# Splitting GpSimd's late bonus products by heads, and summing the last tile's left 256 columns ahead of the right 128

## The chip, the cores and the metric

The kernel runs on one core of one Trainium2 chip. The metric is the time of one execution on the device in microseconds, the median of several runs. A profiled execution shows for each engine what ran when; its span is counted from the first recorded instruction to the last and is a little shorter than the time of a run. TensorE (PE in the profile) multiplies matrices, with weight loads listed apart (PEld); VectorE is DVE, ScalarE is ACT, GpSimd is POOL, and SyncE is SP, here the queue that issues transfers.

## The reference

Two stages follow each other. The first is a linear attention with a decaying state, for 4 sequences of 768 steps, 8 heads of 48 elements:

```
cur = einsum('bhd,bhe->bhde', u * k[t], v[t])
y[t] = einsum('bhd,bhde->bhe', r[t], state + cur)
state = w[t][..., None] * state + einsum('bhd,bhe->bhde', k[t], v[t])
```

The term with u is the bonus of the current step. It can be pulled out of the recurrence: for each step and head it is v[t] times one number, the sum over d of r u k. The second stage is a feed-forward layer on the 3072 rows of 384 columns that come out: h = x @ w_in with 2048 columns, a leaky ReLU with slope 0.01, and g @ w_out back to 384 columns.

## The kernel before, in words

The steps are cut into 24 chunks of 128 (six for each sequence). A chunk's attention is done in parallel form: VectorE, ScalarE and GpSimd make decayed copies of r and k (rk), these are transposed (rkT), TensorE makes scores of 128x128 for each head (L787), VectorE masks them (m, L459), and TensorE sums scores times v and the state's part in a PSUM bank, yp (L817 and L822). Beside this runs the bonus (L402 to L421): ru is r times u (L408), then that times k (L412), VectorE reduces it over each head to dg, one number for each of 8 heads (L416), and the bonus product vs is v times dg spread over 48 elements (L420). All elementwise products go through the helper at L334, which sends them to VectorE or GpSimd. At L490 VectorE adds yp and vs to y, which is transposed into xT (from chunk 12 on by a transfer, L496).

The second stage goes chunk by chunk too. Up: four times 12 matmuls of 128 columns, into a PSUM bank hp (L860), then ScalarE's leaky ReLU to g (L907). Down: four quarters of four matmuls of 384 columns into a PSUM bank op (L928). A copy to o follows on ScalarE or VectorE (L964), and a transfer to the output (L968).

The last chunk, number 23, is special. Its sum lies in two banks: op holds the left 256 columns, and yp, by then free of attention, the right 128 (`last_parts`, L873). In the first three quarters the loop at L926 to L930 does a left and a right matmul in turn for each of four rows of the weights. The fourth quarter is written in two steps (L935 to L944): four left matmuls, then four right ones. Behind each part follows a copy, on ScalarE for the left and on VectorE for the right (L945), and a transfer from SyncE (L950 to L953).

The order in which each engine executes its instructions is fixed in advance. Every piece of work is a step with an engine, a duration that the planner assumes, dependencies and a priority. A planner (`Plan.order`, L40) simulates the engines with these durations and gives out the steps in order of their start; a list written by hand (EARLY, L162) fixes the order of the attention's steps on each engine, and for some of them the engine. P0 is ten times the number of the chunk (L718). Steps with several instructions keep these together. Waits between engines are put in from the data that the instructions touch. Buffers go round in rings: four of vs, three of dg, two of hp.

Of the kernel before, what the change touches and what calls it, by code (L numbers as in the profile page):

```python
# [126 lines left out]
def kernel(  # L127
# [106 lines left out]
    w_out_b = pool.tile([128, NJ, DM], BF16, name="w_out_b")  # L234
# [29 lines left out]
    with tc.manual_schedule():  # L264
# [52 lines left out]
        def step(eng, dur, fn, pri, reads=(), writes=(), deps=(), wire=None, rows=0, **alts):  # L317

            d = list(deps)
            for x in writes:  # L320
                d += x.old
            i = plan.add(eng, dur, fn, d, pri, wire, rows, {eng: dur, **alts} if alts else None)
            for x in (*reads, *writes):
                x.steps.append(i)
            return i

        def copy(e, o, i):
            if e == "ACT":
                nc.scalar.copy(out=o, in_=i)  # L329
            else:  # L330
                (nc.vector if e == "DVE" else nc.gpsimd).tensor_copy(out=o, in_=i)  # L331

        def times(e, o, a, b):
            (nc.vector if e == "DVE" else nc.gpsimd).tensor_tensor(out=o, in0=a, in1=b, op=ALU.mult)  # L334
# [4 lines left out]
        def act(n, src=180):  # L339
            return (src + n) / 1200.0 + 0.02  # L340
# [55 lines left out]
        def product(rk, a, xn, e, P0, deps, banked):  # L396
# [2 lines left out]
                lambda eng: times(eng, rk.t[:, a, :, 0:D], xn.t, e.t[:]),  # L399
                P0, reads=[xn, e], writes=[rk], deps=deps, **({"DVE": 0.58} if banked else {"POOL": 1.05}))  # L400

        def bonus(vs, rn, kn, vn, loads, P0):  # L402

            ru, dg = ru_r.take(), dg_r.take()
            kl, rl, vl = loads
            s_ru = step(
                "POOL", 1.05,
                lambda e: times(e, ru.t[:], rn.t, ubv),  # L408
                P0 + 2, reads=[rn], writes=[ru], deps=[rl, u_ld], DVE=0.84)
            s_ruk = step(  # L410
                "POOL", 1.05,
                lambda e: times(e, ru.t[:], ru.t[:], kn.t),  # L412
                P0 + 2, reads=[kn, ru], deps=[kl, s_ru], DVE=0.84)
            s_dg = step(
                "DVE", 0.54,
                lambda: nc.vector.tensor_reduce(out=dg.t[:], in_=ru.t[:], axis=AX.X, op=ALU.add),  # L416
                P0 + 2, reads=[ru], writes=[dg], deps=[s_ruk])
            return step(
                "POOL", 0.92,
                lambda e: times(e, vs.t[:], vn.t, dg.t[:].unsqueeze(2).to_broadcast([128, H, D])),  # L420
                P0 + 2, reads=[vn, dg], writes=[vs], deps=[vl, s_dg], DVE=0.84)  # L421

        def gt(t):
# [113 lines left out]
        def pair(n):  # L537
# [310 lines left out]
        for nb, size in enumerate(blocks):  # L848
# [24 lines left out]
        def last_parts(op):  # L873

            return (op.t, 0, 256), (side.t, 256, DM)


        seq = []
        for kind, cs, qs in FIRST:
# [3 lines left out]
        for nb in range(4, len(blocks) + 1):  # L883
            a = made[nb][0] if nb < len(blocks) else []
# [12 lines left out]
        for rank, (kind, nb, item) in enumerate(seq):  # L897
            pri = 1000 + rank
            if kind == 0:
                up, j, J, N, g, m_chs, deps = item  # L900
                hp = hp_r.take()
                s_up = step("PE", J * 3 * (N / 2400 + 0.0025), lambda up=up, hp=hp: up(hp), pri,
                            writes=[hp], deps=deps)

                s_g = step(
                    "ACT", act(J * N),
                    lambda hp=hp, g=g, j=j, J=J, N=N: nc.scalar.activation(  # L907
                        out=g.t[:, j : j + J, 0:N],
                        in_=hp.t[:, 0 : J * N].rearrange("p (a n) -> p a n", a=J),
                        func=AF.Prelu, alpha=0.01),  # L910
                    5, reads=[hp], writes=[g] if j == 0 else [], deps=[s_up])
                if j:
                    g.steps.append(s_g)
                for ch in m_chs:
                    up_done.setdefault(ch, s_up)
                for a in range(J):
                    g_done[nb, j + a] = s_g
            else:
                ch, q, g, off = item
                if q == 0:  # L920
                    ops[ch] = op_r.take()
                    side = yp_r.take() if ch == NCH - 1 else None
                op = ops[ch]

                def down(op=op, g=g, q=q, off=off, ch=ch):
                    for j in range(q * NJ // 4, (q + 1) * NJ // 4):  # L926
                        for t, n0, n1 in ((op.t, 0, DM),) if ch < NCH - 1 else last_parts(op):
                            nc.tensor.matmul(  # L928
                                t[:, 0 : n1 - n0], lhsT=g.t[:, j, off : off + 128], rhs=w_out_b[:, j, n0:n1],
                                start=(j == 0), stop=(j == NJ - 1))  # L930
                deps = [g_done[nb, j] for j in range(q * NJ // 4, (q + 1) * NJ // 4)]
                deps += wout_s[q * NJ // 4 // JQ] + ([downs[ch]] if q else [])
                if (ch, q) == (NCH - 1, 3):

                    for part, (t, n0, n1) in enumerate(last_parts(op)):  # L935
                        o = o_r.take()

                        def right(t=t, n0=n0, n1=n1):
                            for j in range(3 * NJ // 4, NJ):
                                nc.tensor.matmul(  # L940
                                    t[:, 0 : n1 - n0], lhsT=g.t[:, j, off : off + 128], rhs=w_out_b[:, j, n0:n1],
                                    start=False, stop=(j == NJ - 1))

                        s_dn = step("PE", 4 * (0.0025 + (n1 - n0) / 2400), right, pri, reads=[g, op, side], deps=deps)  # L944
                        s_o = step(  # L945
                            ("ACT", "DVE")[part], (0.4, 0.28)[part],
                            lambda t=t, n0=n0, n1=n1, o=o, e=("ACT", "DVE")[part]: copy(
                                e, o.t[:, n0:n1], t[:, 0 : n1 - n0]),
                            3, writes=[o], reads=[op, side], deps=[s_dn])
                        step(  # L950
                            "SP", 0.4,
                            lambda n0=n0, n1=n1, o=o: nc.sync.dma_start(out=rows[ch][:, n0:n1], in_=o.t[:, n0:n1]),
                            5, reads=[o], deps=[s_o], wire=(0.4, 0.25)[part], rows=128)  # L953
                    continue
                s_dn = step("PE", 4 * 0.1625, down, pri, reads=[g],
                            writes=([op] if side is None else [op, side]) if q == 0 else [], deps=deps)
                downs[ch] = s_dn
                if q:
                    op.steps.append(s_dn)
                if q == 3:  # L960
                    o = o_r.take()
                    s_o = step(
                        *(("ACT", 0.5) if ch < OACT else ("DVE", 0.56)),
                        lambda e, o=o, op=op: copy(e, o.t[:], op.t[:, 0:DM]),  # L964
                        3, reads=[op], writes=[o], deps=[s_dn], ACT=0.5, DVE=0.56)
# [10 lines left out]
        for rank, word in enumerate(EARLY.split()):  # L976
            i = int(word.rstrip("avp"))
# [50 lines left out]
```

## Time and profile before

| | |
|---|---|
| time, median of 3 runs | 186.97 us (186.71 to 187.37) |
| span of the profiled execution | 184.1 us |
| vs products on GpSimd, whole kernel | 19, mean 855 ns, 16.2 us in all |
| vs products on VectorE | 5 |
| y additions on VectorE (L490) | 24, mean 554 ns |
| down matmuls of 384 columns (L928) | 71.4 us of TensorE |
| up matmuls (L860) | 76.2 us of TensorE |

The page gives for each engine its busy time, its share of the span and the number of its instructions, and below it the span in 40 slices with the busy tenths of each. Then follows the chain of work that ended last, with shares by engine and by line, and the costliest groups of instructions. In rows of the timeline the first number is the start, the second the duration, then engine, line and operation, the tile that is written and the tiles that are read, and how many instructions the row joins; in brackets stands how long the engine had been idle before and what ended that. Matmuls overlap each other, so the duration of a single one is longer than the spacing of their starts.

### The profile page before, as it was taken

How to read it: one execution, taken by the hardware profiler on the slowest of the kernel's cores; microseconds unless marked ns; L12 is line 12 of the kernel's file. 1: busy time of each engine (PE TensorE's matmuls, PEld its weight loads, DVE VectorE, ACT ScalarE, POOL GpSimd, SP SyncE). 2: the span in 40 equal slices, each digit the busy share in tenths (PEclk: the TensorE clock that was granted, in tenths of full speed). 3: DMA queues.
4: the chain of work that ended last, by engine and by line, in shares of the span. 5: the costliest groups of instructions: out<-in, count | busy, mean ns of one | idle time of the engine just before them, and what ended most of it. 6: DMA issues, size and time to landing. Idle time of an engine off the chain costs nothing.

```text
span 184.1 us, 6227 instructions
## 1 busy us (share of the span) xinstructions
PE 175.5 (95%) x2579; PEld 136.5 (74%) x2583; DVE 121.8 (66%) x237; ACT 121.5 (66%) x263; POOL 93.4 (51%) x129
## 2 busy tenths in 40 slices
PE   7977799999999999999999999999999999999992
PEld 2455587877788687789687787886968777877882
DVE  2498585468679878987968768557548588755000
ACT  2784875666787887698957586766657645652660
POOL 7987582552566778789065667313516346110000
PEclk9999999999999999999999999999999999999999
DMA  6999999999999899996885997988989997641202
GB/s 150 261 282 319 348 331 275 266 180 219 221 185 232 167 234 200 227 206 151 174 155 103 135 196 152 212 166 174 191 196 192 169 183 206 162 115 33 66 4 85
DMA packets 120238, 34.62 MB, mean 188 GB/s; under 512 B 109841, under 2 KB 120210, under 8 KB 120210
## 3 DMA queue, kind: packets, MB, share of 16 engines
q1 hardware_dynamic: 120208, 34.22, 84.6%
q8 instruction: 20, 0.33, 0.7%
q14 instruction: 8, 0.07, 0.1%
q10 hardware_dynamic: 2, 0.00, 0.0%
HBM read 25.17 MB, written 4.72 MB: 162 GB/s over the span
## 4 chain that ended last, share of the span: by engine, by line
PE 82%; SPq 10%; DMA 5%; ACT 1%; issue 0%; DVE 0%
PE op L928 34%; PE hp L860 33%; SPq L363 5%; DMA in<-in_moe_w_out_dram 5%; SPq L516 4%; PE se L787 3%; PE yp L822 2%; PE cp L737 2%; PE yp L817 2%; PE yp L798 2%; PE so L441 1%; PE yp L504 1%; PE se L441 1%; PE cp L742 1%; ACT g L907 1%
## 5 line engine op out<-in xcount | busy, mean ns | idle before, releaser
L907 ACT ACTIVATE g<-hp 128x512 bf16<-128x512 f32 x96 | 56.8, 596 | 35.3 <-PE hp L860 33.4
L860 PE MATMUL hp<-xT,w_in_b 128*128 128x128 bf16 x1152 | 76.2, 219 | 1.4 <-ACT w_in_b L329 0.9
L860 PEld LDWEIGHTS <-w_in_b 128*128 128x128 bf16 x1152 | 67.4, 98 | 6.4 <-ACT w_in_b L329 1.2
L928 PE MATMUL op<-w_out_b,g 128*128 128x384 bf16 (+1 forms) x380 | 71.4, 324 | 0.2 <-ACT g L907 0.2
L928 PEld LDWEIGHTS <-g 128*128 128x128 bf16 x392 | 34.8, 98 | 17.8 <-DVE w_out_b L331 0.3
L334 POOL TENSOR_TENSOR ru<-in,ub 128x384 f32<-128x384 f32 x19 | 19.1, 1010 | 11.7 <-DMA in<-in_r_dram 8.1
L334 POOL TENSOR_TENSOR rk<-in,ek 128x384 bf16<-128x384 f32 x15 | 15.6, 1038 | 17.2 <-ACT ek L393 15.9
L334 POOL TENSOR_TENSOR vs<-in,dg 128x384 f32<-128x384 f32 x19 | 16.2, 855 | 14.2 <-DVE dg L416 11.1
L490 DVE TENSOR_TENSOR y<-yp,vs 128x384 bf16<-128x384 f32 x24 | 13.3, 554 | 13.1 <-PE yp L822 9.6
L334 POOL TENSOR_TENSOR ru<-ru,in 128x384 f32<-128x384 f32 x15 | 15.6, 1043 | 3.9 <-DMA in<-in_k_dram 2.3
L334 POOL TENSOR_TENSOR sb<-s,a 128x384 bf16<-128x384 f32 x13 | 11.3, 867 | 11.9 <-DVE s L479 5.1
L459 DVE TENSOR_TENSOR m<-se,maskb 128x512 bf16<-128x512 f32 x20 | 13.7, 684 | 3.6 <-PE so L787 3.3
L459 DVE TENSOR_TENSOR m<-so,maskb 128x512 bf16<-128x512 f32 x20 | 13.7, 684 | 3.2 <-PE so L787 3.2
L383 ACT ACTIVATE lw<-in 128x384 bf16<-128x384 f32 x24 | 12.3, 519 | 3.3 <-DMA in<-in_w_dram 3.3
L334 DVE TENSOR_TENSOR rk<-in,cp 128x384 bf16<-128x384 f32 x22 | 12.0, 547 | 3.1 <-ACT cp L393 2.1
L752 DVE TENSOR_TENSOR ci<-cp,lw 128x384 f32<-128x384 f32 x20 | 11.1, 553 | 3.8 <-PE cp L742 3.5
L416 DVE TENSOR_REDUCE dg<-ru 128x8 f32<-128x384 f32 x24 | 13.0, 544 | 0.2
L329 ACT COPY o<-op 128x384 f32<-128x384 f32 (+1 forms) x16 | 7.5, 471 | 6.5 <-PE op L928 5.1
L479 DVE TENSOR_TENSOR s<-yp,sb 128x384 f32<-128x384 f32 x14 | 7.8, 554 | 5.2 <-PE yp L798 4.3
L393 ACT ACTIVATE cp<-cp 128x384 f32<-128x384 f32 x22 | 10.5, 478 | 0.6 <-DVE ci L752 0.3
L393 ACT ACTIVATE ek<-ci 128x384 f32<-128x384 f32 x20 | 10.4, 518 | 0.4 <-DVE ci L752 0.2
L787 PE MATMUL se<-rkT 48*128 48x128 bf16 x80 | 7.9, 219 | 0.0
(125 smaller groups left out, 220.7 us busy)
## 6 DMA issues: line engine op xcount, KB each, us to landing
out_dram<-o SPq DMA_DIRECT2D x23, 192.0 KB, 3.2
in<-in_w_dram SPq DMA_DIRECT2D x20, 192.0 KB, 4.0
in<-in_r_dram SPq DMA_DIRECT2D x20, 192.0 KB, 3.8
in<-in_k_dram SPq DMA_DIRECT2D x20, 192.0 KB, 3.8
in<-in_v_dram SPq DMA_DIRECT2D x20, 192.0 KB, 3.8
in<-in_moe_w_in_dram SPq DMA_DIRECT2D x8, 384.0 KB, 7.6
in<-in_moe_w_out_dram SPq DMA_DIRECT2D x8, 384.0 KB, 7.5
in<-in_w_dram SPq DMA_DIRECT2D x2, 384.0 KB, 5.0
```

The source lines that it names most:

```text
L334: (nc.vector if e == "DVE" else nc.gpsimd).tensor_tensor(out=o, in0=a, in1=b, op=ALU.mult)
L363: "SP", 0.45, lambda part=part, src=src: nc.sync.dma_start(out=part, in_=src), pri,
L383: lambda: nc.scalar.activation(out=lw.t[:, :, 0:D], in_=wn.t, func=AF.Ln),
L393: "ACT", 0.5, lambda: nc.scalar.activation(out=out.t[:], in_=i, func=AF.Exp, scale=scale),
L416: lambda: nc.vector.tensor_reduce(out=dg.t[:], in_=ru.t[:], axis=AX.X, op=ALU.add),
L459: lambda par=par: nc.vector.tensor_tensor(out=m.t[:, par], in0=gt(sc[par].t), in1=mask.unsqueeze(1).to_broadcast([128, NP, 128]), op=ALU.m ...
L490: lambda: nc.vector.tensor_tensor(out=y.t[:], in0=hd(yp.t[:, 0:DM]), in1=vs.t[:], op=ALU.add),
L752: lambda: nc.vector.tensor_tensor(out=ci.t[:], in0=hd(cp.t[:, 0:DM]), in1=lw.t[:, :, 0:D], op=ALU.add),
L787: nc.tensor.matmul(gt(sc[par].t)[:, p, :], lhsT=rkT.t[q0 : q0 + D, NP + p, :], rhs=rkT.t[q0 : q0 + D, p, :], start=True, stop=True, skip_g ...
L860: nc.tensor.matmul(hp.t[:, a * N : (a + 1) * N], lhsT=w_in_b[:, t, (j + a) * 128 : (j + a + 1) * 128], rhs=xT[:, t, c0 : c0 + N], start=(a ...
L907: lambda hp=hp, g=g, j=j, J=J, N=N: nc.scalar.activation(out=g.t[:, j : j + J, 0:N], in_=hp.t[:, 0 : J * N].rearrange("p (a n) -> p a n", ...
L928: nc.tensor.matmul(t[:, 0 : n1 - n0], lhsT=g.t[:, j, off : off + 128], rhs=w_out_b[:, j, n0:n1], start=(j == 0), stop=(j == NJ - 1))
```

## The change

It has two parts.

The first is in `bonus`. Where the planner has put a bonus product on GpSimd and the chunk is number 12 or later (P0 of 120 or more), four instructions of two heads each, 128x96, take the place of one of 128x384. The result is the same. It is meant to have GpSimd occupy what it shares with VectorE for shorter stretches at a time. The planner's assumed duration stays.

The second concerns the last chunk's down. The left and the right sum no longer go side by side: the first two quarters do only left matmuls, the third does its left ones and then the right ones of the first two quarters, and the fourth step pair does the left ones of the last quarter and then the right ones of the last two. So the left 256 columns are complete with eight right matmuls still to come, instead of four. It is meant to let the copy and the transfer of the larger part begin earlier. The assumed durations follow.

```diff
+        def by_heads(e, o, a, b, parts):
+            for i in range(parts):
+                hs = slice(i * H // parts, (i + 1) * H // parts)
+                times(e, o[:, hs, :], a[:, hs, :], b[:, hs].unsqueeze(2).to_broadcast([128, H // parts, D]))
...
             return step(
                 "POOL", 0.92,
-                lambda e: times(e, vs.t[:], vn.t, dg.t[:].unsqueeze(2).to_broadcast([128, H, D])),
+                lambda e: by_heads(e, vs.t, vn.t, dg.t, 4 if e == "POOL" and P0 >= 120 else 1),
...
+        def quarters(op, g, off, which):
+            for part, q in which:
+                t, n0, n1 = last_parts(op)[part]
+                for j in range(q * NJ // 4, (q + 1) * NJ // 4):
+                    nc.tensor.matmul(
+                        t[:, 0 : n1 - n0], lhsT=g.t[:, j, off : off + 128], rhs=w_out_b[:, j, n0:n1],
+                        start=(j == 0), stop=(j == NJ - 1))
...
-                def down(op=op, g=g, q=q, off=off, ch=ch):
+                def down(op=op, g=g, q=q, off=off, last=last):
+                    if last:
+                        quarters(op, g, off, ((0, q),) if q < 2 else ((0, 2), (1, 0), (1, 1)))
+                        return
...
-                        s_dn = step("PE", 4 * (0.0025 + (n1 - n0) / 2400), right, pri, reads=[g, op, side], deps=deps)
+                        s_dn = step(
+                            "PE", (0.44, 0.46)[part],
+                            lambda op=op, g=g, off=off, qs=(((0, 3),), ((1, 2), (1, 3)))[part]: quarters(op, g, off, qs),
+                            pri, reads=[g, op, side], deps=deps)
...
-                s_dn = step("PE", 4 * 0.1625, down, pri, reads=[g],
+                s_dn = step("PE", 4 * 0.1625 if not last else (0.44, 0.44, 0.9)[q], down, pri, reads=[g],
```

More of the change, by code (lines that the diff above doesn't have):

```diff
@@ L923 @@
                 op = ops[ch]
-                def down(op=op, g=g, q=q, off=off, ch=ch):
+                last = ch == NCH - 1
+                def down(op=op, g=g, q=q, off=off, last=last):
+                    if last:
+                        quarters(op, g, off, ((0, q),) if q < 2 else ((0, 2), (1, 0), (1, 1)))
+                        return
                     for j in range(q * NJ // 4, (q + 1) * NJ // 4):
[L927 to L930, printed above, removed]
+                        nc.tensor.matmul(
+                            op.t[:, 0:DM], lhsT=g.t[:, j, off : off + 128], rhs=w_out_b[:, j, :],
+                            start=(j == 0), stop=(j == NJ - 1))
                 deps = [g_done[nb, j] for j in range(q * NJ // 4, (q + 1) * NJ // 4)]
                 deps += wout_s[q * NJ // 4 // JQ] + ([downs[ch]] if q else [])
-                if (ch, q) == (NCH - 1, 3):
+                if last and q == 3:
                     for part, (t, n0, n1) in enumerate(last_parts(op)):
                         o = o_r.take()
[L938 to L942, printed above, removed]
-                        s_dn = step("PE", 4 * (0.0025 + (n1 - n0) / 2400), right, pri, reads=[g, op, side], deps=deps)
+                        s_dn = step(
+                            "PE", (0.44, 0.46)[part],
+                            lambda op=op, g=g, off=off, qs=(((0, 3),), ((1, 2), (1, 3)))[part]: quarters(op, g, off, qs),
+                            pri, reads=[g, op, side], deps=deps)
                         s_o = step(
```

## The prediction

> **What bounds the kernel now.** I read the page's busy table and its slices first, then the chain, then the waits of TensorE, then the timeline of the last microseconds. The page says which engine is full and from when:
>
> ```profile
> PE 175.5 (95%) x2579; PEld 136.5 (74%) x2583; DVE 121.8 (66%) x237; ACT 121.5 (66%) x263; POOL 93.4 (51%) x129
> PE   7977799999999999999999999999999999999992
> POOL 7987582552566778789065667313516346110000
> PE 82%; SPq 10%; DMA 5%; ACT 1%; issue 0%; DVE 0%
> ```
>
> TensorE is full from the seventh slice (some 28 us) until 181; GpSimd is half idle and, over the last third, mostly idle. "Busy" of TensorE is modelled, so I looked at it in two more ways. Asked for the waits of TensorE from 30 us on, the trace names none. And from 30 us to 181 I compared the start of each group of matmuls with the next start and with its columns at 2.4 a nanosecond: no gap exceeds that by over 0.15 us, and the 25 that exceed it by 0.1 or more sum to 2.9 us, spread evenly and mostly at a change of matmul shape. So between 30 us and the end the time is the sum of TensorE's instructions in their fixed order. The other engines matter only if one makes TensorE wait, or after its last matmul. What follows the last matmul is in the timeline (start, duration, engine, line):
>
> ```profile
> 179.99 0.60 PE L940 MATMUL op<-w_out_b,g 128*128 128x256 bf16 x4
> 180.42 0.39 PE L940 MATMUL yp<-w_out_b,g 128*128 128x128 bf16 x4
> 180.62 0.37 ACT L329 COPY o<-op 128x256 f32<-128x256 f32 x1 [1.28 <-PE op L940]
> 180.85 0.29 DVE L331 COPY o<-yp 128x128 f32<-128x128 f32 x1 [10.64 <-PE yp L940]
> 181.02 0.81 SPq L952 DMA_DIRECT2D out_dram<-o  x2
> ```
>
> The left 256 columns are complete at 180.59, ScalarE copies them until 180.99, and SyncE issues their transfer at 181.02. VectorE has the right 128 columns in SBUF at 181.14, but their transfer is the second of two issues that take 0.81 us together, and by the view of the output tensor the last one starts at 181.4. From there to the end of the span, 184.07, only the transfer and the closing remain. So the second issue waits for SyncE, and SyncE was held up by the left part, which came last.
>
> **What the skill says.** The Trainium skill, "SBUF — State Buffer", section "Who interferes with whom", says that a VectorE instruction with two SBUF inputs and a GpSimd instruction that reads SBUF exclude each other for the whole instruction. The trace agrees: a VectorE product that takes 0.54 us alone took 0.94 from 97.20, with a bonus product on GpSimd from 96.90 to 97.73, and 0.75 from 152.53 beside the one from 152.02. Those 0.40 and 0.21 us are all that I find behind the nine products in question; this is what shorter instructions could give back. "Perfetto Trace Analysis", section "GPSIMD Engine Instruction", advises to time GpSimd by the spacing of starts. Here it is 0.79 us (vs at 152.02, the next at 152.81) against a reported 0.83.
>
> **The first edit: nine bonus products in four pieces.** The order of GpSimd's program has nine products with P0 of 120 or more on this engine (the products of chunks 13, 15 and 17 are on VectorE and stay whole). They become 36 instructions of 128x96; nothing else moves on GpSimd, VectorE, ScalarE or SyncE.
>
> ```profile
> L334 POOL TENSOR_TENSOR vs<-in,dg x9: 827/828/874, 86.0 to 158.4; 128x384 f32<-128x384 f32 x9
> ```
>
> No GpSimd product of 96 columns is in the trace. Bound from below: no fixed cost, four pieces take the 0.79 us of one. Bound from above: the selections at the start of the kernel took 236 ns for 64 columns and 293 for 128, so 0.89 ns a column and 179 ns fixed; three more of those give 0.79 + 3 x 0.18 = 1.33 us. Between them stands the price of "GPSIMD Engine Reference", section 3.1: 4497 ns for 2048 columns at 2.6 cycles each of 1.2 GHz leaves 60 ns fixed, so an estimate of 0.79 + 0.18 = 0.97 us. I take 1.0, which is 0.2 us more each and 1.9 us of GpSimd in all, between 0 and 4.9.
>
> Is any of it on TensorE's path? The sum is read by the y instruction of its chunk (L490). By the order of the ring of four vs buffers the nine pair up with the y starts as follows, end of vs then start of y: 86.9 and 98.6, 97.7 and 110.7, 109.6 and 124.1, 129.9 and 137.8, 130.9 and 143.6, 142.2 and 150.8, 152.9 and 159.4, 156.4 and 165.9, 159.3 and 169.7. The smallest slack is 6.5 us against 0.54 at worst. Queued behind the pieces is GpSimd's next instruction. In seven cases of nine GpSimd then idled for something else (1.12, 0.56, 0.15, 3.29, 2.04 and 2.91 us, and 3.17 after one more product), which swallows 0.2; the 0.15 leaves 0.05 over, and the 3.17 behind it takes that. The two others lead to a ru product, from 86.83 and from 152.81. The first is wanted at 91.35. The second ends at 154.13 and would end at 154.33; a VectorE product (rk) stands beside it under the lock until 154.54 and may slip by as much. Its transpose is issued at 155.63, behind another issue, takes a median 4.2 us to land, so about 159.8, and is read by TensorE at 161.95. Slack 2 us. So this edit costs nothing, hidden behind TensorE. It also gains nothing: the 0.6 us of lock on VectorE is no time of TensorE.
>
> **The second edit: the last tile's order on TensorE.** The same 16 matmuls of 256 columns and 16 of 128, each with its weight load, in another order: nothing is removed or added. Before, the fourth quarter's left part was followed by four narrow matmuls only; now by eight. The chain of waits has the steps:
>
> ```profile
> 180.15 0.44 PE op L940 x4
> 180.59 0.24 PE yp L940 x4
> 180.82 0.02 issue
> 180.85 0.29 DVE o L331
> ```
>
> Four narrow matmuls more are 4 x 0.0557 us, with 0.67 us for 12 of that shape in the chain's rows of L860. The left sum is complete at 180.59 - 0.22 = 180.37. ScalarE copies from 180.40 to 180.77, SyncE issues at 180.80, and the second issue follows at 181.22 instead of 181.44. Its data is ready at 181.14 + 0.03, as before, since TensorE's last matmul stays at 180.83; so SyncE still sets it, with 0.05 us to spare (a gain beyond 0.27 would meet that limit). The end comes 0.22 us sooner.
>
> What could take it back: the first quarter's four narrow matmuls no longer stand ahead of the last two groups of L860, so these start at 176.47 instead of 176.68. Their buffers were freed by ScalarE's pair of 1.27 us that started at 174.90 and ended at 176.17, so they are not late. Each quarter's g is done a microsecond or more before it is read (the last pair ends at 178.82, the last quarter's left part starts at 179.94).
>
> **Sum.** 186.97 + 0 - 0.22 = 186.75 us.
>
> **Rivals.**
>
> A, narrow matmuls in a row are dearer. "TensorE: Matmul & The Clock Gate", section "Back-to-back issue gap", gives 81 ns for a sustained pair of load and 128-column matmul. Two rows of eight at 81 instead of 56 ns would add 0.4 us to TensorE while the left part still gains: the right part's data would come at 181.57 and the end at 184.07 + 0.16, so 187.1. The trace speaks against it: L860 is exactly such a row, and takes 0.67 for 12, 1.34 for 24.
>
> B, slower: the pieces are dear and reach TensorE. If each cost the upper bound and VectorE took the lock between pieces (0.55 us each time), the busy stretch from 150 to 157 us could slip by 1 to 2.5 us, against 2 us of slack at the score matmuls; TensorE would stand for about 0.7 us and the time be 187.5. Against it stands that GpSimd idles 1.43 us in that stretch, and every other product has more room.
>
> C, the relief of the lock counts. If the 0.6 us of VectorE, or a shorter wait that I don't see, sat on TensorE's path, it would add up to 0.6 to the gain: 186.2. Against it: no wait of TensorE after 30 us.
>
> **How the numbers follow.** My forecast (tail gain of 0.1 to 0.27, the rest hidden) has 0.78, A 0.06, B 0.08, C 0.08. The three runs of before lie between 186.71 and 187.37, so 0.3 us is left to chance on each side. 0.3% is 0.56 us: faster needs 186.41, slower 187.53. The forecast lies within it but for a tenth on the near side; A within; C beyond it in half its cases, B in three quarters. Faster: 0.08 + 0.04 = 0.12. Slower: 0.06. Same: the remaining 0.82. The range goes from 186.3, which takes in half of C, to 187.4, which takes in A and the mild half of B.
>
> **What would show it.** Right: 36 vs instructions of some 0.25 us, GpSimd's busy time up by 1 to 3 us, VectorE's slow products at 97 and 152 us shorter, TensorE's busy time and the start of its last matmul unchanged; ScalarE's last copy about 0.2 us earlier before the end, the two issues closer behind it, and a wait of the second copy unchanged. Wrong: any wait of TensorE after 30 us, a score matmul that waits for rkT, a last row of eight narrow matmuls that takes over 0.5 us, or a last issue that starts later than 0.05 us after VectorE's copy is done and yet not earlier than before.

## The result, and the profile after

| | before | after |
|---|---|---|
| median of the timed runs, 6 each (the first three of before are those known ahead) | 186.84 us (186.56 to 187.48) | 186.06 us (185.84 to 186.15) |
| ratio, with its 95% interval | | 0.995 (0.9931 to 0.9969) |
| time of the profiled run | 186.2 us | 185.94 us |
| span of the profiled run | 184.07 us | 183.90 us |

The forecast was 186.75 us with a range from 186.3 to 187.4, so the time fell below the range. The table already holds the puzzle of this case: the medians differ by 0.78 us, the two profiled runs by only 0.26, and their spans by 0.17.

I first compared the pages. These rows of the page of after answer to those shown of before (busy times, slices of TensorE and GpSimd, shares of the chain):

```profile
PE 176.8 (96%) x2583; PEld 137.2 (75%) x2583; DVE 121.4 (66%) x237; ACT 121.2 (66%) x263; POOL 98.2 (53%) x156
PE   7998799999999999999999999999999999999993
POOL 7987583552566778788267676313816257410000
PE 82%; SPq 10%; DMA 5%; ACT 1%; issue 0%; DVE 0%
```

TensorE is full over the same slices, the shares of the chain are the same to the percent, and GpSimd has 27 instructions more (9 whole ones replaced by 36) and is busy 4.8 us longer. Nothing here looks like 0.8 us.

The timeline of after's last microseconds (start, duration, engine, line) shows the second edit at work, and the chain its steps:

```profile
179.82 0.60 PE L886 MATMUL op<-w_out_b,g 128*128 128x256 bf16 x4
180.25 0.61 PE L886 MATMUL yp<-w_out_b,g 128*128 128x128 bf16 x8
180.45 0.37 ACT L329 COPY o<-op 128x256 f32<-128x256 f32 x1 [1.28 <-PE op L886]
180.85 0.81 SPq L965 DMA_DIRECT2D out_dram<-o  x2
180.90 0.29 DVE L331 COPY o<-yp 128x128 f32<-128x128 f32 x1 [10.64 <-PE yp L886]
```

```profile
179.98 0.44 PE op L886 x4
180.42 0.46 PE yp L886 x8
180.88 0.02 issue
180.90 0.29 DVE o L331
```

(The rows of before stand in the prediction.) ScalarE's copy of the left part starts 0.45 us ahead of VectorE's copy of the right one, instead of 0.23; the first issue starts 0.05 us ahead of VectorE's copy instead of 0.17 behind its start; and the second issue starts 0.09 us after that copy is done, where it was 0.31. That is the 0.22 us of the prediction.

To find where the rest went I cut both spans at VectorE's y additions (L490 before, L495 after), of which each chunk has one, so that they lie all along the kernel. "Third y" is the start of the third of them, and so on:

| us | third y | third to fifth | fifth to last | last y to end | span |
|---|---|---|---|---|---|
| before | 29.32 | 16.34 | 123.99 | 14.41 | 184.07 |
| after | 29.45 | 16.26 | 124.00 | 14.19 | 183.90 |

The last y, of before and then of after, is in these rows:

```profile
169.65 0.56 DVE L490 TENSOR_TENSOR y<-yp,vs 128x384 bf16<-128x384 f32 x1 [1.20 <-issue]
169.71 0.56 DVE L495 TENSOR_TENSOR y<-yp,vs 128x384 bf16<-128x384 f32 x1 [1.20 <-issue]
```

The long middle part is equal to 0.01 us, though all nine split products lie in it. The end is 0.22 shorter. The first 46 us differ by 0.05, in the other direction. So inside the spans the profiled pair shows the change forecast and no more. Of the 0.26 us between its times, 0.09 lie outside the spans; the further half microsecond of the medians is between runs that were timed and not profiled. This became the question for the experiments.

### The profile page after: what moved, and what is told of

It reads as the page before. It is cut to its first block, busy times and chain, and to the rows that moved or that the text cites. A ratio compares the mean times of both kernels' runs of the same rounds, so it can differ in the third digit from the quotient of the medians.

```text
span 183.9 us, 6258 instructions
## 1 busy us (share of the span) xinstructions
PE 176.8 (96%) x2583; PEld 137.2 (75%) x2583; DVE 121.4 (66%) x237; ACT 121.2 (66%) x263; POOL 98.2 (53%) x156
## 4 chain that ended last, share of the span: by engine, by line
PE 82%; SPq 10%; DMA 5%; ACT 1%; issue 0%; DVE 0%
PE op L945 33%; PE hp L865 33%; SPq L363 5%; DMA in<-in_moe_w_out_dram 5%; SPq L521 4%; PE se L792 3%; PE yp L827 2%; PE cp L742 2%; PE yp L822 2%; PE yp L803 2%; PE yp L509 1%; PE se L446 1%; PE so L446 1%; PE op L886 1%; PE cp L747 1%; ACT g L920 1%
## 5 line engine op out<-in xcount | busy, mean ns | idle before, releaser
L945 PE MATMUL op<-w_out_b,g 128*128 128x384 bf16 x368 | 69.6, 326 | 0.2 <-ACT g L920 0.2
L945 PEld LDWEIGHTS <-g 128*128 128x128 bf16 x368 | 32.9, 98 | 17.4 <-DVE w_out_b L331 0.3
L334 POOL TENSOR_TENSOR vs<-in,dg 128x96 f32<-128x96 f32 (+1 forms) x46 | 20.8, 479 | 13.6 <-DVE dg L421 8.4
L495 DVE TENSOR_TENSOR y<-yp,vs 128x384 bf16<-128x384 f32 x24 | 13.3, 555 | 13.5 <-PE yp L827 9.9
L1004 PE MATMUL op<-zeros 128*128 128x512 bf16 (+1 forms) x19 | 7.6, 459 | 1.3 <-DVE zeros L302 1.3
```

The lines of the kernel that those rows point to most:

```text
L495: lambda: nc.vector.tensor_tensor(out=y.t[:], in0=hd(yp.t[:, 0:DM]), in1=vs.t[:], op=ALU.add),
L945: nc.tensor.matmul(op.t[:, 0:DM], lhsT=g.t[:, j, off : off + 128], rhs=w_out_b[:, j, :], start=(j == 0), stop=(j == NJ - 1))
```

## The experiments

Every experiment was timed beside runs of the kernel before on the same chip, and each result below names the median of those. In the expectations the theories go by letters. They come down to these: the change is worth its tail alone (about 0.2 us) and the rest of the first comparison is spread of the runs; or it is worth the 0.8 us that the comparison showed, by a wait that the split takes away in most runs and not in the profiled one.

### Before against itself, the second edit alone, the first edit alone

The kernel before, unchanged, shows what a comparison with nothing in it gives:

> The kernel before, unchanged, as a control. Its six runs lay between 186.56 and 187.48 us while its profiled run took 186.2, and those of the changed kernel between 185.84 and 186.15. Theory S (a stall in the middle of the kernel before that comes in most of its runs but not in the profiled one, and that the split removes): runs again spread over about 1 us, median 186.8, and a trace of a slow one has a wait of TensorE after 30 us. Theory T (the tail alone is the cause and the spread is chance): median 186.3 to 186.5, no wider than 0.4 us. Theory L (the spread comes from the loads of the first 30 us): spread as before, and the first y of a late trace is late from the start.

The second edit alone is the changed kernel with whole products:

```diff
-                lambda e: by_heads(e, vs.t, vn.t, dg.t, 4 if e == "POOL" and P0 >= 120 else 1),
+                lambda e: by_heads(e, vs.t, vn.t, dg.t, 1),
```

> Only the last tile's order is changed; all bonus products stay whole. Theory S: 186.6 us, with the spread of the kernel before, since only 0.2 us of the gain is of the tail. Theory T: 186.06, as with both parts, within 0.15. Theory L: 0.2 us below the control, with its spread.

The first edit alone is the kernel before with the split products:

```diff
-                lambda e: times(e, vs.t[:], vn.t, dg.t[:].unsqueeze(2).to_broadcast([128, H, D])),
+                lambda e: by_heads(e, vs.t, vn.t, dg.t, 4 if e == "POOL" and P0 >= 120 else 1),
```

> Only the nine bonus products are split; the last tile is as before. Theory S: 186.3 us and a narrow spread of 0.3 us, the gain of 0.5 to 0.6 us being of the split. Theory T: as the control, within 0.15 us. Theory L: as the control, with its spread.

| | median us, runs | ratio, interval | third to fifth y | last y to end |
|---|---|---|---|---|
| before, beside them | 186.33, 41 | | | |
| before again | 186.18, 13 | 1.0002 (0.999 to 1.0015) | 16.16 | 14.41 |
| second edit alone | 186.12, 21 | 0.9994 (0.9984 to 1.0003) | 16.18 | 14.19 |
| first edit alone | 186.14, 13 | 0.9995 (0.9982 to 1.0007) | 16.17 | 14.40 |

Neither edit alone gives 0.8 us, and both theories that put it into one of the edits fall. What had moved was the kernel before: 41 runs with a median of 186.33, where the first comparison had 6 with 186.84 and the time known ahead was 186.97. The spread of about a microsecond stayed (185.89 to 187.04 for before again), so the narrow one that theory T expected isn't there either. Inside the span the traces give each edit its own share: 0.22 us for the second edit, none for the first.

The first edit does take something off outside it. For every run the record has the time and the span (to 0.1 us). The time less the span averages 2.12 us over the 41 runs of before and 2.13 with the second edit alone, but 2.04 with the first edit alone: 0.08 us that the trace of the span can't show.

In the trace of the first edit alone the fifth y to the last took 124.20 instead of 124.00. The waits of TensorE's weight loads (engine, line, waited for: us in total, times, longest) name one more, and the timeline has the chain behind it:

```profile
PEld L933 <- ACT g L912: 0.2, 1, 0.2
```

```profile
151.45 0.55 DVE L334 TENSOR_TENSOR rk<-in,cp 128x384 bf16<-128x384 f32 x1 [0.15 <-DMA in<-in_r_dram]
152.04 0.17 ACT L780 ACTIVATE a<-cp 64x4 f32<-64x4 f32 x1 [0.87 <-DVE rk L334]
152.23 1.25 ACT L912 ACTIVATE g<-hp 128x512 bf16<-128x512 f32 x2
```

VectorE's rk product waited 0.15 us for a load of r, ScalarE's small activation for that product, and the leaky ReLU queued behind it was late for the down matmuls. No instruction of the edit is in this chain. The load landed late in this run and not in the others, and it reached TensorE far into the kernel. It pointed to loads as something that makes runs differ.

### The changed kernel again, a further step of each edit, and a late load

If loads that land late are the spread, a load that is made late should cost what it is late by, and the changed kernel should lie about 0.2 us below before on a new chip. First the changed kernel as it is:

> The changed kernel once more, beside fresh runs of the kernel before on the same chip. Theory W (the change is worth 0.2 us by the tail, and the first comparison was wide of it because the runs of the kernel before vary by a microsecond from run to run, and six of them had fallen high): ratio 0.999, within 0.998 to 0.9997. Theory D (the two parts together give what neither gives alone): ratio 0.995 again, 0.8 us.

The second edit taken to its end: all 16 left matmuls, then all 16 right ones.

```diff
-                        quarters(op, g, off, ((0, q),) if q < 2 else ((0, 2), (1, 0), (1, 1)))
+                        quarters(op, g, off, ((0, q),))
...
-                            "PE", (0.44, 0.46)[part],
-                            lambda op=op, g=g, off=off, qs=(((0, 3),), ((1, 2), (1, 3)))[part]: quarters(op, g, off, qs),
+                            "PE", (0.44, 0.92)[part],
+                            lambda op=op, g=g, off=off, qs=(((0, 3),), ((1, 0), (1, 1), (1, 2), (1, 3)))[part]: quarters(op, g, off, qs),
```

> The changed kernel with all sixteen left matmuls of the last tile ahead of all sixteen right ones. Theory Q (the second issue on SyncE sets the end, and VectorE's copy is the next limit): ScalarE's copy 0.45 us earlier than with the change, but the last issue only as much earlier as it stands behind VectorE's copy now, 0.05 us; time within 0.1 us of the changed kernel. If the left copy alone set the end: 0.45 us faster.

The first edit doubled, with eight pieces of one head:

```diff
-                lambda e: by_heads(e, vs.t, vn.t, dg.t, 4 if e == "POOL" and P0 >= 120 else 1),
+                lambda e: by_heads(e, vs.t, vn.t, dg.t, 8 if e == "POOL" and P0 >= 120 else 1),
```

> The changed kernel with the nine products in eight pieces, one head each. By the 0.305 us spacing of a piece of 96 columns and 0.79 of a whole product, a piece of 48 costs 0.22 us, a product 1.8 us: 0.6 us more than with four pieces, 5 us of GpSimd in all. Theory H (the products are hidden behind TensorE): the time of the changed kernel within 0.2 us, no new wait of TensorE over 0.2 us. Theory N (they are not): 0.5 us slower or more.

And an extra load of 384 KB, into a tile that nothing reads, ahead of the first load of w_out:

```diff
+                def load(part=part, src=src, extra=(which, q, half) == (1, 0, 0)):
+                    if extra:
+                        nc.sync.dma_start(out=spare[:], in_=src)
+                    nc.sync.dma_start(out=part, in_=src)
```

> The changed kernel with one load of 384 KB more, into a tile that nobody reads, ahead of the first load of w_out. At some 300 GB/s it takes 1.3 us of the queues. Theory L (the start of TensorE's full stage, set by the loads of the first 28 us, moves the end one for one): 1.0 to 1.5 us slower, every step from 30 us on shifted by the same. If the loads had slack: no change.

| | median us, runs | ratio, interval | third y | third to fifth | last y to end |
|---|---|---|---|---|---|
| before, beside them | 186.23, 61 | | | | |
| changed kernel | 186.02, 22 | 0.9994 (0.9983 to 1.0005) | 29.32 | 16.21 | 14.18 |
| all left, then all right | 185.76, 22 | 0.998 (0.9972 to 0.9988) | 29.32 | 16.15 | 14.06 |
| eight pieces | 185.89, 20 | 0.9984 (0.9975 to 0.9992) | 29.38 | 16.19 | 14.18 |
| late load | 186.96, 6 | 1.0038 (1.0025 to 1.0052) | 30.38 | 16.16 | 14.27 |

The changed kernel is 0.21 us below before. All left first is another 0.26 below it by the medians and 0.13 us in the trace, where the issue alone promised 0.05. Its tail in the timeline:

```profile
179.57 1.06 PE L886 MATMUL yp<-w_out_b,g 128*128 128x128 bf16 x16
179.77 0.37 ACT L329 COPY o<-op 128x256 f32<-128x256 f32 x1 [0.83 <-PE op L886]
180.17 1.15 SPq L965 DMA_DIRECT2D out_dram<-o  x2
180.67 0.29 DVE L331 COPY o<-yp 128x128 f32<-128x128 f32 x1 [10.64 <-PE yp L886]
```

Now the first issue is over before VectorE's copy is, and the second issue starts 0.03 us after the copy: SyncE bounds nothing any more. Of the 0.13 us, 0.06 come from that (0.09 behind the copy became 0.03), 0.07 from a shorter way from the last issue to the end of the span (2.54 us where all others have 2.60 to 2.62); the issue itself took 0.33 instead of 0.38.

The eight pieces cost nothing either, though they have GpSimd busy 103.8 us. The late load costs 0.94 us over the changed kernel beside it, just under the 1.0 to 1.5 expected, and its trace has it all before the third y, with TensorE's weight loads waiting from 28 us on as follows:

```profile
PEld L953 <- DVE w_out_b L334: 1.5, 1, 1.5
```

The third y came 1.06 us later than in the changed kernel beside it (30.38 against 29.32). So what this load holds TensorE up by in the first 30 us comes out at the end nearly in full.

### Which load in the spread, and a narrower right part

On a third chip, the kernel before (and one further profiled run of it), the changed kernel, and a right part of 64 columns with all left matmuls first:

> The kernel before once more as a control, for its spread. Theory W: median 186.1 to 186.4 with single runs up to 187, ratio 1. Theory D (something of the first comparison's chip makes the kernel before slow there): median 186.7 to 187 if that comes back.

> One more trace of the kernel before, in the hope of a run above 186.5 us. If the excess is in the loads of the start, the fifth y comes later than 45.9 us; if it is in the middle, the time from the fifth to the last y exceeds 124.0 us and a wait of TensorE shows, as in the trace with the split alone, where a late load of r cost 0.2 us at 152; if it is in the tail, the time from the last y to the end exceeds 14.4 us.

> The changed kernel beside it. Theory W: 0.2 us below the kernel before, ratio about 0.999, with single runs up to 187 too. Theory D: 0.8 us below and no run above 186.3.

```diff
-            return (op.t, 0, 256), (side.t, 256, DM)
+            return (op.t, 0, 320), (side.t, 320, DM)
```

(with whole products, and the planner's durations 0.54 and 0.5)

> A version that may beat both: bonus products whole, all left matmuls of the last tile ahead of the right ones, and the right part 64 columns wide instead of 128. VectorE's last copy handles half as much: [...]the last issue comes 0.07 us earlier than with 128 columns, if rows of 64-column matmuls cost no more than 27 ns each and the smaller transfer lands no later. From the last y to the end 14.0 us, against 14.06 with 128 columns, 14.19 with the change and 14.41 before; median 185.7 to 185.8 where the kernel before takes 186.2.

| | median us, runs | ratio, interval | profiled run | third to fifth y | last y to end |
|---|---|---|---|---|---|
| before, beside them | 186.31, 45 | | | | |
| before again | 186.34, 14 | 1.0 (0.9989 to 1.0011) | 186.5 | 16.55 | 14.41 |
| before, one further run | 186.15, 1 | | 186.15 | 16.34 | 14.42 |
| changed kernel | 185.91, 22 | 0.9976 (0.9965 to 0.9987) | 186.29 | 16.61 | 14.19 |
| right part of 64 columns | 185.90, 15 | 0.998 (0.9968 to 0.9992) | 185.96 | 16.27 | 14.14 |

The two profiled runs that were high, 186.5 of before and 186.29 of the changed kernel, gave what I had lacked: traces of long runs. Both lose their time between the third and the fifth y, and there the waits of TensorE's weight loads name one cause in both; the first row is of the kernel before, the second of the changed one:

```profile
PEld L441 <- POOL rk L334: 0.5, 1, 0.5
```

```profile
PEld L446 <- POOL rk L334: 0.6, 1, 0.6
```

The timeline of the kernel before in that run has the chain:

```profile
37.53 0.82 POOL L331 CAST w_out_b<-in 128x768 bf16<-128x768 f32 x1 [1.06 <-DMA in<-in_moe_w_out_dram]
38.11 0.66 DVE L334 TENSOR_TENSOR ru<-ru,in 128x384 f32<-128x384 f32 x1 [0.71 <-DMA in<-in_k_dram]
38.48 1.14 POOL L334 TENSOR_TENSOR rk<-in,ek 128x384 bf16<-128x384 f32 x1
39.68 0.23 PEld L441 LDWEIGHTS <-rk 128*128 128x128 bf16 x4 [0.50 <-POOL rk L334]
```

GpSimd waits for one of the last loads of w_out, casts it, then makes the rk of chunk 4 from k, and TensorE stands for that. VectorE was idle for 0.71 us just before, waiting for the same k. And the trace of before that the prediction was read from has the same row, with 0.4 us. Of the five traces of before only the one with the shortest way from third to fifth y, 16.16 us, has no such row:

```profile
PEld L441 <- POOL rk L334: 0.4, 1, 0.4
```

I had asked for the waits of TensorE's matmuls. In that trace it is the weight load that carries the wait, and the matmul rows name none.

The right part of 64 columns missed its 14.0 us (14.14). 16 such matmuls take only 0.48 us in the chain, 30 ns each, but the left part is wider, and its copy takes longer:

```profile
180.38 0.48 PE yp L886 x16
```

```profile
180.22 0.63 PE L886 MATMUL yp<-w_out_b,g 128*128 128x64 bf16 x16
180.42 0.43 ACT L329 COPY o<-op 128x320 f32<-128x320 f32 x1 [1.15 <-PE op L886]
180.87 0.81 SPq L965 DMA_DIRECT2D out_dram<-o  x2
180.89 0.22 DVE L331 COPY o<-yp 128x64 f32<-128x64 f32 x1 [10.64 <-PE yp L886]
```

The first issue comes at 180.87, so the second is bound by SyncE again, as before the change. The 256 and 128 of the kernel, all left first, are better by 0.08 us in the traces.

### Taking the wait away, and making it worse

If rk on GpSimd behind a late cast is a cause of the spread, moving it to VectorE should lower the median and the upper runs of the kernel before. In the handwritten order (EARLY) a "v" puts a product on VectorE, a "p" on GpSimd; 157 is rk of chunk 4, 163 the ru product:

```diff
-        143p 149 739 158 163v 179 157p 755 740 759 164 756 180 160 159 182 762 760 184 209 306 745 763v
+        143p 149 739 158 157v 163v 179 755 740 759 164 756 180 160 159 182 762 760 184 209 306 745 763v
```

> The kernel before with one product moved: rk = k times ek of chunk 4 from GpSimd, behind a cast of w_out that waits for a load, to VectorE, ahead of the ru product. Theory J (the spread of the kernel before comes from the landing of the loads of 34 to 38 us, which reaches TensorE through this product): the wait of TensorE for rk of 0.4 us near 39 us is gone, the fifth y comes at 45.4 to 45.6 in any run, median 0.1 to 0.3 us below the kernel before, runs above 186.6 rarer. If the spread is from elsewhere: same median and spread as the kernel before.

The same move, with whole products and all left matmuls first, puts together what had helped:

> The same move, all bonus products whole, and the last tile's left matmuls all ahead of the right ones. From the last y to the end 14.06 us; by theory J in all 0.35 plus 0.1 to 0.3 us below the kernel before, 185.6 to 185.8, and below the changed kernel on the same chip.

And the extra load of 384 KB again, in the kernel before, this time just ahead of one of the late loads of w_out:

```diff
+                def load(part=part, src=src, extra=(which, q, half) == (1, 3, 0)):
+                    if extra:
+                        nc.sync.dma_start(out=spare[:], in_=src)
+                    nc.sync.dma_start(out=part, in_=src)
```

> The kernel before with one load of 384 KB more, into a tile that nobody reads, ahead of the last load of w_out but one of its halves. Theory J: the load of k behind it and the cast on GpSimd come about 1.2 us later, TensorE waits 1.3 to 1.7 us for rk near 39 us instead of 0.4, and the end comes 0.9 to 1.3 us later. If these loads had slack: no change.

> The changed kernel again, beside the same runs of the kernel before. Theory W: ratio about 0.999 (0.998 to 0.9995). Theory D: 0.995.

| | median us, runs | ratio, interval | third to fifth y | last y to end |
|---|---|---|---|---|
| before, beside them | 186.29, 43 | | | |
| rk on VectorE | 185.92, 22 | 0.998 (0.9971 to 0.9988) | 16.16 | 14.41 |
| rk on VectorE, all left first, whole products | 185.52, 6 | 0.9949 (0.9935 to 0.9964) | 16.16 | 14.05 |
| late load of w_out | 187.41, 4 | 1.0053 (1.0033 to 1.0072) | 17.02 | 14.51 |
| changed kernel | 186.06, 22 | 0.9989 (0.9979 to 0.9999) | 16.19 | 14.41 |

With rk on VectorE the wait for it is gone. In the timeline of that kernel it starts at 37.53, in the gap that VectorE had, where GpSimd started it at 38.13 in the first trace of before and at 38.48 in the long one:

```profile
37.53 0.63 DVE L334 TENSOR_TENSOR rk<-in,ek 128x384 bf16<-128x384 f32 x1 [0.88 <-DMA in<-in_k_dram]
38.09 0.54 DVE L334 TENSOR_TENSOR ru<-ru,in 128x384 f32<-128x384 f32 x1
```

The median fell by 0.37 us, and of 22 runs one lies above 186.6, of 43 of before seven. But little of that is the wait. The time less the span averages 1.84 us with rk on VectorE and 2.13 in the runs of before beside it, so 0.29 us went outside the span. The spans themselves average 184.11 against 184.20, a difference of 0.09 that is not clear of their scatter, and spans of 184.5 or more are 2 of 22 against 7 of 43. What lies outside is not in the traces, but for one thing: in all eight traces of kernels with whole bonus products and this rk on GpSimd, one transfer of the queue q14, which the page lists as one of instructions, starts 1.7 us after the span's end, and in the twelve others none does. This is its row for the kernel before, in the view of transfers from 184.1 to 187 us:

```profile
q14 instruction: 1, 0.01, 1.2%
```

It does not tell the 2.04 us of the split products from the 1.84, so why the time outside the span differs stays open.

The late load of w_out gave the opposite of a removal. The same wait grew from 0.4 to 1.0 us, less than the 1.3 to 1.7 expected, and the time by 1.1:

```profile
PEld L449 <- POOL rk L337: 1.0, 1, 1.0
```

Its growth accounts for 0.6 us of the 1.1; the profiled run was the shortest of the four, at 187.06. So this wait, when it grows, reaches the end, and the traces of long runs have it. That it makes a large part of the spread of the timed runs is not shown: taking it away left their spans nearly as they were. (In both kernels with an extra load the way from the last issue to the end was 0.1 us longer as well; why was not pursued.)

In the trace of the changed kernel here the last y to the end took 14.41, as before the change. It isn't the tail that failed: from VectorE's last copy to the end everything is as in the other traces. TensorE stood for 0.23 us at 169.5, in front of the first up matmuls of chunk 22, and all later times moved with it. The row names only "issue", but the transposed x of that chunk landed late:

```profile
166.61 1.97 SPq L501 DMA_TRANSPOSE xT<-y  x1
169.74 0.54 PEld L865 LDWEIGHTS <-w_in_b 128*128 128x128 bf16 x9 [0.16 <-issue]
```

This transfer landed 3.1 us after its start, at 169.7, where TensorE went on; in the six other traces with this last tile it took 2.3 to 2.8 us. So here too a transfer that landed late set the time.

### Once more on a fifth chip

Before, the changed kernel and the combined kernel again:

> The kernel before as a control, a fourth time. Theory W: median 186.1 to 186.4. Theory D: on a chip like that of the first comparison, 186.7 to 187.

> The changed kernel beside it. Theory W: 0.2 us below the kernel before by the tail, give or take 0.15 of the spread. Theory D: 0.8 us below where the kernel before is at 186.8.

> The version with the product of chunk 4 on VectorE, whole bonus products and all left matmuls first, a second time: 0.35 us by the tail and 0.1 to 0.3 by the product below the kernel before, ratio 0.9965 to 0.998 if its first six runs had fallen low, 0.995 if they had not; below the changed kernel by 0.2 us or more.

| | median us, runs | ratio, interval | third to fifth y | last y to end |
|---|---|---|---|---|
| before, beside them | 186.26, 23 | | | |
| before again | 186.35, 13 | 1.0002 (0.9989 to 1.0015) | 16.40 | 14.40 |
| changed kernel | 185.94, 11 | 0.999 (0.9973 to 1.0006) | 16.16 | 14.19 |
| combined | 185.49, 5 | 0.995 (0.9934 to 0.9965) | 16.28 | 14.05 |

The combined kernel beats both: 0.77 us below before on two chips, and 0.54 and 0.45 below the changed kernel beside it. Of the 0.77 us, 0.3 lies outside the span again: the time less the span averages 1.81 and 1.84 us in its runs. Its spans are 0.53 and 0.55 us shorter than those of before, on average, of which the tail has 0.36; the rest, between third and fifth y, is not settled by five and six runs. In the second trace that stretch took 16.28 us without any wait for rk, so rk is not all that moves it.

## Why the prediction was wrong

**The tail is worth what was forecast.** The step "the end comes 0.22 us sooner" held to 0.01: 14.40 to 14.42 us from last y to end in seven traces with the old tail (the kernel before five times, the first edit alone, rk on VectorE), 14.18 or 14.19 in six with the new one (the changed kernel four times, the second edit alone, the eight pieces). The exceptions are the two kernels with an extra load and the one trace with a wait of TensorE ahead of the tail. Over four later comparisons the changed kernel lay 0.21, 0.40, 0.23 and 0.32 us below before, by medians, and their four ratios average to 0.9987, which is 0.24 us. That this is so near to 0.22 is in part luck: the spans alone are 0.16 us shorter on average (0.05 to 0.34 in the single comparisons), and 0.08 us are time outside the span, which the "+ 0" of the first edit did not have. Before against itself gave -0.15, +0.03 and +0.09, so one such comparison can be off by 0.1 to 0.15.

**The step that failed is the base of the sum, "186.97 + 0 - 0.22", and the allowance of "0.3 us left to chance on each side".** On five chips 213 runs of the kernel before have a median of 186.26 (185.84 to 187.40), and each chip lies between 186.23 and 186.33. Only 34 of them, 16%, are at 186.56 or more, while all six of the first comparison are, the three known ahead among them. Their times differ by up to 1.6 us, while the time less the span stays between 2.06 and 2.18, so the spread is inside the span; it is not the granted clock, which was full in 22 of those 34 and in 149 of all 213. From 186.26 the sum gives 186.04, and the changed kernel measured 186.06 first and 185.97 over 77 later runs. Of the 0.78 us of the first comparison, some 0.2 is the change and some 0.6 the height of the six runs of before. There had been a hint: the profiled run took 186.2, at least 0.5 below each of the three times. The tail, the middle and the start were all read from that run, so the sum should have started from it: 186.2 - 0.22 = 185.98, against 185.94 for the profiled run of after.

**The second step that failed is "the trace names none".** It was right of the rows that I asked for and wrong of the kernel. On the weight loads stood 0.4 us for GpSimd's rk, beside eleven waits of some 0.32 us each at the score matmuls, which are the same in the other traces of before. It would have been a reason to ask when loads of w_out and k land, and how far that can move the time with no change at all. The forecast of the change itself does not suffer, since none of its instructions lies there.

**The nine products.** They cost nothing, as forecast: fifth y to last y is 123.99 or 124.00 with and without them, and with eight pieces too. But the price of "0.2 us more each" was too low. By the timeline of GpSimd (starts count, the durations overlap) four pieces take 1.21 us, from 108.83 to 110.04, where a whole one took 0.79:

```profile
108.83 1.25 POOL L334 TENSOR_TENSOR vs<-in,dg 128x96 f32<-128x96 f32 x4
110.04 1.00 POOL L334 TENSOR_TENSOR ru<-in,ub 128x384 f32<-128x384 f32 x1
```

That is 0.42 us more, inside the bound of 0.54, where nothing stands beside it; nine of these would be 3.8 of GpSimd's 4.8 us. Eight pieces take 1.78 us. So one more instruction costs 0.14 us both times. Beside VectorE's products the pieces took longer than the bound allowed: 1.53 us from 152.09 to the start of the ru product, 0.74 more than a whole one, so that this product ended at 154.94 and not at the 154.33 forecast. It stayed within the 2 us of slack.

```profile
152.09 1.57 POOL L334 TENSOR_TENSOR vs<-in,dg 128x96 f32<-128x96 f32 x4
153.62 1.32 POOL L334 TENSOR_TENSOR ru<-ru,in 128x384 f32<-128x384 f32 x1
```

**The lock.** These are VectorE's products before, and then after:

```profile
97.20 0.94 DVE L334 TENSOR_TENSOR sb<-s,a 128x384 bf16<-128x384 f32 x1
152.53 0.75 DVE L334 TENSOR_TENSOR ru<-ru,in 128x384 f32<-128x384 f32 x1
153.66 0.88 DVE L334 TENSOR_TENSOR rk<-in,ek 128x384 bf16<-128x384 f32 x1
154.47 0.54 DVE L334 TENSOR_TENSOR sb<-s,a 128x384 bf16<-128x384 f32 x1
```

```profile
97.25 0.55 DVE L334 TENSOR_TENSOR sb<-s,a 128x384 bf16<-128x384 f32 x1
152.58 0.57 DVE L334 TENSOR_TENSOR ru<-ru,in 128x384 f32<-128x384 f32 x1
153.54 0.54 DVE L334 TENSOR_TENSOR rk<-in,ek 128x384 bf16<-128x384 f32 x1
154.00 1.35 DVE L334 TENSOR_TENSOR sb<-s,a 128x384 bf16<-128x384 f32 x1
```

The two slow products that the prediction named are quick now, as forecast. GpSimd's ru product, which stood beside rk before, moved to stand beside sb, so rk is quick too and sb is slow. The four together took 3.11 us and take 3.01. That VectorE's relief is worth no time of TensorE held.

**The rivals.** A fell: eight narrow matmuls took 0.46 us, and "a last row of eight narrow matmuls that takes over 0.5 us" was the sign against. B fell: no load or matmul waits for a product made of pieces, nor for what stands behind one. C would have named the measured time, 186.2 and below, but for a reason that did not happen: the split alone shortens no part of the trace, and the 0.08 us that it takes off lie outside the span.

**What stays open** is why all six runs of before in the first comparison lay high. On five chips that did not come back, and the chip of the first comparison is not on record. That there the kernel before was slower and the changed one was not, by something that the change takes away, is not excluded; the one profiled run of before from that time, 186.2, speaks against it. The rk wait explains up to 0.45 us above the shortest way from third to fifth y in a trace; that it lifted those six is not shown, and the spans with rk on VectorE speak against its being most of it. Open too is what shortens the time outside the span, by 0.08 us with the split products and by 0.3 with rk of chunk 4 on VectorE.

## What to carry to other kernels

Start the sum from the run that the trace shows when the timed runs disagree with it, and take the spread for what it is: cut two traces at an instruction that recurs all along the kernel, and an effect of 0.2 us stands out to 0.01 where the medians of six runs move by 0.6. Then compare the time less the span as well: moving one product to another engine shortened it by 0.3 us here, and the median alone would have put that down to a wait. Ask for the waits of TensorE's weight loads, not only of its matmuls. At the end of a kernel with two output parts, have the larger one complete so early that its issue is over when the smaller one's data is ready.

## What I had not expected of the hardware

- **Many short GpSimd instructions.** Each further one in a row costs 0.14 us where VectorE does not stand beside it. From the Trainium skill, "GPSIMD Engine Reference", section 3.1, I had worked out an estimate of 60 ns; the measurement decides. The mean of the pieces in the page's groups by form, 369 ns each, times four is 1.48 us and overstates even that, since they overlap:

```profile
L334 POOL TENSOR_TENSOR vs<-in,dg 128x96 f32<-128x96 f32 x36 | 12.1, 369 | 8.2 <-DMA in<-in_v_dram 5.2 <-DVE dg L421 2.9
```

- **The lock moves.** Shorter GpSimd instructions did let VectorE in between, as the section "Who interferes with whom" of "SBUF — State Buffer" has it that they exclude each other for a whole instruction; but the total of the four hardly fell (3.11 to 3.01 us), since the pieces last longer and what follows them collides elsewhere.
- **Narrow matmuls.** A row of eight pairs of load and 128-column matmul takes 0.46 us, 57 ns each, where "TensorE: Matmul & The Clock Gate", section "Back-to-back issue gap", has 81. Sixteen of 64 columns took 0.48 us in the chain of the narrow right part, 30 ns each.
- **Time outside the span.** It is constant to about 0.1 us for one kernel and differs between kernels: 2.06 to 2.18 us for before, 1.79 to 1.92 with one product of chunk 4 on another engine.
- **Landings.** Between profiled runs of the same kernel the third y moved by 0.15 us (29.27 to 29.42 in five traces of before) and the two chunks after it by 0.4 (16.16 to 16.55), while from the fifth y on 19 chunks repeated to 0.01 us unless one load came late.
